# Chunked attention with a gated MLP on one core: scratch products ahead, row sums on TensorE, another order of loads

## The chip, the core and the metric

The kernel runs on one core of a Trainium2 chip (trn2). A core has TensorE (PE in the rows, with its weight loads as PEld), VectorE (DVE), ScalarE (ACT), GpSimd (POOL) and SyncE (SP), which here only starts transfers. Each engine works through its own queue in order and waits at the head of it. The metric is the device time of the one core in microseconds; lower is better.

## The reference

Attention first: each chunk of 32 queries sees 8 memory keys and the 56 keys from 16 before the chunk to 8 behind it, 64 in all.

```
scores = (q_c @ k_full.T) / sqrt(64)          # k_full: 8 memory keys, then 56 keys of the context
scores = scores - max(scores)
a      = exp(scores);  a = a / (sum(a) + 1e-9)
out_c  = a @ v_full
```

The heads are then put side by side (4 batches, 768 tokens, 512 columns), and a gated MLP follows:

```
h = relu(x @ w_in);  u, v = halves of h                     # 512 -> 1024
v = (v - mean(v)) / sqrt(var(v) + 1e-6)
g = u * (w_spatial @ v + b_spatial)                         # mixes the 768 tokens of a batch
out = g @ w_out                                             # 512 -> 512
```

Heads 8, head size 64. The MLP's weights arrive as 64-bit floats.

## The kernel before, in words

Attention runs in 24 units, six a batch: a unit is 4 chunks, so 128 queries, of all 8 heads. For unit i TensorE makes the scores (line L491, into the PSUM tile sx, of which there is one); DVE takes the row maximum (L558) and subtracts it into p (L562); ACT takes exp (L567); TensorE transposes p (L590, tile pt), ACT copies that to SBUF (L593, pT); TensorE multiplies with v (L491, "f<-vmain,pT", called P in the prediction, into a bank of tile f or into sx); DVE has meanwhile summed p and inverted the sum (L572, L573, L575) and scales the result into xs (L540 or L535); TensorE transposes it (L605, xt), ACT writes the high part of x (L610) and DVE the low part (L614). From unit 3 on (SPLIT) one burst makes the scores of unit i and the P of unit i-1 together.

The MLP's products carry each operand as a high and a low part (rounded to the type fp32r and the rest), so each product is three: the high parts of both (L642), the left one's low with the right one's high (L643), and the left one's high with the right one's low (L644); for v the left one is x, for u it is w_in. Such a triple is the unit of TensorE's work. For one token tile, v takes four triples of 512 columns ("f<-win_h,x", one for each 128 rows of w_in), u takes four triples of 384 columns for a block ("f<-x,win_h"), the token mixing takes six ("f<-wsp_h,vn") and the last product four ("f<-wout,big").

A block of 128 rows and 512 columns of w_in is converted from 64 bits by a chain over three engines: ACT takes the high word's value (L795) and the low word's (L800), DVE puts in exponent and sign (L804, L805), POOL adds (L810), ACT rounds to the high part win_h (L813), and DVE or POOL takes the low part win_l (L817). (c, 1) is the block of rows c for v, (c, 0) that for u. The raw blocks lie in tile big, with four buffers; a fifth load waits until the first buffer's add is done.

The operands of v come in two layers: 32 rows straight from memory, and 24 rows that are the next chunk's first rows, which for the first batch are copied on the chip by `shift_v` (L431, on ACT or POOL). P of a unit needs its copies.

`Plan` sets the order of everything. Each step is recorded with its engine (or a choice of engines with a cost for each), a cost, what it reads and writes, and a rank; the planner then lets time run, starts on each engine the step that can start first (the lowest rank among equals), and writes the instructions in that order. The order is fixed when the program is built; the hardware then waits by semaphores. The list FIRST gives the first loads in the order in which SP starts them, with conversion and load ranks for the w_in blocks. SP starts a load only when the loads ahead of it that are still under way would stay below AHEAD bytes.

The v of the MLP is normalized by POOL's power (L680), DVE's subtract and multiply (L684), ACT's rounding to the high part (L687) and DVE's low part (L691).

## Time and profile before

| | us |
|---|---|
| runs: median (lowest to highest, three) | 401.56 (400.12 to 403.46) |
| the profiled execution's own time | 403.73 |
| its span from first to last instruction | 402.0 |
| TensorE busy | 370.0 (92%) |
| DVE busy | 209.0 (52%) |
| ACT busy | 155.6 (39%) |
| POOL busy | 101.1 (25%) |

The busy shares are means over the whole span, and the span has two very different stretches. In the first 35 us data arrive, weights are converted and the first units pass through their chain, and TensorE has little to do; from about 92 us on TensorE works almost without a break. The table by stages in the prediction shows this. Of the profile's kinds of rows, those of the timeline give start, duration, engine, line and operation, and in brackets how long the engine stood idle before and what it waited for; those of groups give count, total busy time and the mean in ns.

### The profile page before, as it was taken

Reading aid. Unit: us, or ns where it says so; the run is one execution under the profiler, and the core shown is the slowest. Engines: PE = TensorE matmul, PEld = TensorE weight load, DVE = VectorE, ACT = ScalarE, POOL = GpSimd, SP = SyncE. Lnnn points to the kernel's source line nnn. Section 1 sums busy time; section 2 is a strip of 40 time slices with the busy share of each in tenths; the row PEclk is TensorE's granted clock in tenths of the full one; section 3 lists DMA queues with packets and bytes.
Section 4 is the critical chain, followed back from the end, with each engine's and each line's share of the span. In section 5 each row is a group of like instructions: output and inputs, shape, how many; then the busy total and the mean of one; then the engine's idle time right before and its main releaser. Section 6 shows DMA issues by size and latency. Waiting matters only on the chain.

```text
span 402.0 us, 11030 instructions
## 1 busy us (share of the span) xinstructions
PE 370.0 (92%) x4812; PEld 331.0 (82%) x4812; DVE 209.0 (52%) x401; ACT 155.6 (39%) x276; POOL 101.1 (25%) x114
## 2 busy tenths in 40 slices
PE   1458889889999999999999999999999999999996
PEld 0346777788989878889987988989989889899895
DVE  2799998897753525394661323475421324414040
ACT  6576765754342234344333222334211223321212
POOL 4786575332202101020121110110221201103031
PEclk9979999999999999999999999999999999999999
DMA  7889458861336450023736210000001020000202
GB/s 252 223 263 303 162 138 202 242 200 49 121 118 203 127 183 33 0 49 128 176 72 214 67 50 30 2 2 3 0 7 73 2 79 0 2 0 2 78 3 78
DMA packets 29505, 39.54 MB, mean 98 GB/s; under 512 B 5392, under 2 KB 23568, under 8 KB 29456
## 3 DMA queue, kind: packets, MB, share of 16 engines
q1 hardware_dynamic: 29152, 38.73, 32.1%
q8 instruction: 38, 0.62, 0.7%
q10 hardware_dynamic: 304, 0.10, 0.1%
q14 instruction: 11, 0.09, 0.1%
HBM read 32.52 MB, written 6.29 MB: 97 GB/s over the span
## 4 chain that ended last, share of the span: by engine, by line
PE 76%; DMA 13%; DVE 4%; ACT 3%; SPq 1%; issue 1%; POOL 1%; ACTq 0%; POOLq 0%
PE f L642 22%; PE f L644 22%; PE f L643 22%; PE sx L491 6%; DMA big<-in_moe_w_out_dram 3%; DMA big<-in_moe_w_in_dram 3%; DMA k<-in_k_dram 3%; PE xt L605 2%; PE pt L590 2%; DMA vmain<-in_mem_v_dram 1%; SPq L283 1%; DMA q<-in_q_dram 1%; DMA vmain<-in_v_dram 1%; DVE win_l L817 1%; POOL st L810 1%
## 5 line engine op out<-in xcount | busy, mean ns | idle before, releaser
L740 POOL TENSOR_TENSOR st<-st,u 128x384 f32<-128x384 f32 x32 | 33.7, 1056 | 141.9 <-DVE st L736 101.5
L642 PE MATMUL f<-wsp_h,vn 128*128 128x384 f32 x192 | 66.1, 344 | 0.0
L644 PE MATMUL f<-wsp_l,vn 128*128 128x384 f32 x192 | 64.5, 336 | 0.0
L643 PE MATMUL f<-wsp_h,vn 128*128 128x384 f32 x192 | 64.3, 335 | 0.0
L736 DVE TENSOR_TENSOR st<-f,bias 128x384 f32<-128x384 f32 x32 | 17.6, 553 | 54.5 <-PE f L644 54.4
L642 PE MATMUL f<-x,win_h 128*128 128x384 f32 x128 | 44.1, 345 | 0.5 <-issue 0.5
L643 PE MATMUL f<-x,win_l 128*128 128x384 f32 x128 | 43.0, 336 | 0.5 <-DVE win_l L817 0.5
L644 PE MATMUL f<-x,win_h 128*128 128x384 f32 x128 | 43.0, 336 | 0.0
L680 POOL TENSOR_TENSOR rstd<-ve,mhalf 128x1 f32<-128x1 f32 x24 | 15.5, 646 | 106.4 <-DVE ve L676 106.4
L743 ACT CAST big<-st 128x384 fp32r<-128x384 f32 x32 | 16.4, 512 | 64.5 <-POOL st L740 64.5
L642 PE MATMUL f<-win_h,x 128*128 128x512 f32 x96 | 39.6, 412 | 0.0
L644 PE MATMUL f<-win_l,x 128*128 128x512 f32 x96 | 37.9, 395 | 1.2 <-POOL k L261 1.2
L642 PE MATMUL f<-wout,big 128*128 128x512 f32 (+1 forms) x100 | 38.9, 389 | 0.0
L643 PE MATMUL f<-wout,big 128*128 128x512 f32 (+1 forms) x100 | 38.3, 383 | 0.0
L644 PE MATMUL f<-wout,big 128*128 128x512 f32 (+1 forms) x100 | 38.2, 382 | 0.0
L643 PE MATMUL f<-win_h,x 128*128 128x512 f32 x96 | 37.8, 394 | 0.0
L642 PEld LDWEIGHTS f<-wsp_h,vn 128*128 128x128 f32 x192 | 36.1, 188 | 1.3
L643 PEld LDWEIGHTS f<-wsp_h,vn 128*128 128x128 f32 x192 | 36.1, 188 | 0.7
L491 PEld LDWEIGHTS sx<-k,q 64*32 64x32 f32 x1536 | 17.6, 111 | 22.5 <-issue 12.5
L644 PEld LDWEIGHTS f<-wsp_l,vn 128*128 128x128 f32 x192 | 36.0, 188 | 0.0
L491 PE MATMUL sx<-k,q 64*32 64x64 f32 x1536 | 21.6, 235 | 15.5 <-POOL k L261 9.8
L672 DVE BATCH_NORM_STATS2 stats<-st 128x6 f32<-128x512 f32 x24 | 16.3, 681 | 27.8 <-ACT st L668 27.7
(75 smaller groups left out, 670.8 us busy)
## 6 DMA issues: line engine op xcount, KB each, us to landing
out_dram<-st SPq DMA_DIRECT2D x23, 256.0 KB
k<-in_k_dram SPq DMA_DIRECT2D x7, 800.0 KB
q<-in_q_dram SPq DMA_DIRECT2D x7, 768.0 KB
vmain<-in_v_dram SPq DMA_DIRECT2D x38, 128.0 KB
big<-in_moe_w_in_dram SPq DMA_DIRECT2D x8, 512.0 KB
vmain<-in_v_dram SPq DMA_DIRECT2D x35, 96.0 KB
big<-in_moe_w_spatial_dram SPq DMA_DIRECT2D x6, 384.0 KB
big<-in_moe_w_out_dram SPq DMA_DIRECT2D x4, 512.0 KB
```

What stands on the lines that cost most here:

```text
L283: me["ins"] = e.dma_start(out=dst() if callable(dst) else dst, in_=src_).ins
L491: nc.tensor.matmul(o, w_, m, start=True, stop=True, skip_group_check=True)
L590: nc.tensor.transpose(a[:, t], p[:, t], ident)
L605: nc.tensor.transpose(a[:, t], xs[:, t], ident)
L642: nc.tensor.matmul(o, lh, rh, start=(j == 0), stop=False)
L643: nc.tensor.matmul(o, ll, rh, start=False, stop=False)
L644: nc.tensor.matmul(o, lh, rl, start=False, stop=(j == len(pairs) - 1))
L672: nc.vector.bn_stats(stats, t_["st", s])
L680: nc.gpsimd.tensor_tensor(a, t_["ve", i], mhalf, op=ALU.pow)
L736: nc.vector.tensor_tensor(alloc("st", s_, [P, HT], F32), t_["f", n], bias[:, tok], op=ALU.add)
L740: nc.gpsimd.tensor_tensor(a, a, t_["u", i], op=ALU.mult)
L743: nc.scalar.copy(t_["g", i][:, 0, 0:HT], t_["st", s_])
```

## The change

The new program differs in these points.

- The low parts of w_in and w_out (L817) are now always POOL's (WLOW has only POOL); before, DVE or POOL took them.
- The sums of p of units 0, 1 and 2 are made by TensorE: four products of the transposed p with a matrix `halves` of two columns put the sums of the two heads of a pair beside the unit's P in the same PSUM bank. DVE adds the small constant and inverts (`recip`); its reduction (L572) is left out for these three units.
- The first batch's six normalizations of v are done by ACT (an activation with scale and bias) in place of DVE; DVE makes the bias (`shifts`), one column.
- 28 scratch products of 512 columns (`heat`), whose result nobody reads, stand in TensorE's queue among the first units: 7 ahead of unit 0's scores, 4 behind them, 10 behind unit 1's scores, 7 behind unit 1's transpose.
- SPLIT is 3, so that the scores of unit 3 and P of unit 2 are two steps.
- The first loads come in another order, v in pieces of 3, 1 and 2 units (before 2, 1, 2 and 1), AHEAD is 2,000,000; two of the blocks of w_in are converted only behind the step p of unit 0 and of unit 4 (gate). The copies of keys may go to ACT in the first batch.
- The planner's costs differ, it models a slow and a fast clock of TensorE (`Clock`), and so all orders move.
- Functions with the conditions PSUB and XLOW (both 0) make no instructions. The transposes of xs are written as products with the transpose flag; they are the same four instructions.

TensorE's queue at the start of the program, before. In the names pt is the transposed p, sx the scores, xt the transposed xs; "f<-vmain,pT" is P.

```order
L491 MATMUL sx<-k,q 32x64 x64
L590 MATMUL pt<-ident,p 128x128 x4
L491 MATMUL sx<-k,q 32x64 x32
L590 MATMUL pt<-ident,p 128x128 x4
L491 MATMUL f<-vmain,pT 32x64 x64
L605 MATMUL xt<-ident,xs 128x128 x4
L590 MATMUL pt<-ident,p 128x128 x4
L642 MATMUL f<-win_h,x 128x512
```

The same place now, from the first scratch product to P of unit 1; "xt<-minus" is a scratch product and "f<-halves,pT" the sums of p.

```order
L306 MATMUL xt<-minus 128x512 x7
L546 MATMUL sx<-k,q 32x64 x32
L306 MATMUL xt<-minus 128x512 x4
L682 MATMUL pt<-ident,p 128x128 x4
L546 MATMUL sx<-k,q 32x64 x32
L306 MATMUL xt<-minus 128x512 x10
L546 MATMUL sx<-k,q 32x64 x32
L546 MATMUL f<-halves,pT 128x2 x4
L546 MATMUL f<-vmain,pT 32x64 x32
L682 MATMUL pt<-ident,p 128x128 x4
L306 MATMUL xt<-minus 128x512 x7
L546 MATMUL f<-halves,pT 128x2 x4
```

Before, the scores of units 0 and 1 stood together ahead of unit 0's transpose; now unit 1's scores stand behind it, and the scratch products lie between.

POOL's queue from its first add to the low part of the last of v's four blocks, before. st_233 is block (0,1), st_243 (3,1), st_319 (2,1), st_257 (1,1).

```order
L810 TENSOR_TENSOR st_233<-st_233,big_148 128x512
L431 COPY vmain_113<-vmain_113 24x4x256 x2
L810 TENSOR_TENSOR st_243<-st_243,big_184 128x512
L431 COPY vmain_113<-vmain_113 24x4x256 x2
L810 TENSOR_TENSOR st_319<-st_319,big_236 128x512
L810 TENSOR_TENSOR st_257<-st_257,big_192 128x512
L360 MEMSET k1_143 128x4x16
L484 COPY k_429<-memT_112 128x16x8
L261 COPY k1_143<-k1_143 128x16x24
L817 TENSOR_TENSOR win_l_108<-st_257,win_h_107 128x512
```

The same place now, without its first three rows (the adds of st_219 and st_227 and one copy of 24x4x192). st_227 is block (0,1), st_219 (1,1), st_279 (3,1), st_276 (2,0), st_459 (2,1).

```order
L486 COPY vmain_113<-vmain_113 24x4x256
L935 TENSOR_TENSOR win_l_108<-st_227,win_h_107 128x512
L486 COPY vmain_113<-vmain_113 24x4x192
L415 MEMSET k1_158 128x4x16
L928 TENSOR_TENSOR st_279<-st_279,big_214 128x512
L935 TENSOR_TENSOR win_l_108<-st_219,win_h_107 128x512
L935 TENSOR_TENSOR win_l_108<-st_279,win_h_107 128x512
L928 TENSOR_TENSOR st_276<-st_276,big_208 128x512
L928 TENSOR_TENSOR st_459<-st_459,big_294 128x512
L539 COPY k_569<-memT_112 128x16x8
L935 TENSOR_TENSOR win_l_108<-st_276,win_h_107 128x512
L935 TENSOR_TENSOR win_l_108<-st_459,win_h_107 128x512
```

Of the low parts of v's blocks POOL had one and now has all four, and a fifth, of u's block (2,0), stands ahead of the last of them.

The diff, cut to its core:

```diff
-AHEAD = 1800000
-SPLIT = 2
-FIRST = [("qk", 0, (0, 0), 1), ("qk", 0, (1, 2), 2), ("mem", 0, "ACT", True), ("w", 0, 1, -6.0, 2.0),
...
+AHEAD = 2000000
+SPLIT = 3
+FIRST = [("qk", 0, (0, 0), 1), ("mem", 0, "ACT", True), ("qk", 0, (1, 2), 2), ("w", 1, 1, 40.0, 3.0),
+         ("w", 0, 1, -39.0, 2.0), ("w", 2, 0, 50.0, 27.0), ("w", 3, 1, 49.0, 5.0, 0), ("v", 0, 3, False),
...
+HOT = (7, 4, 3, 7, 7, 0, 0)
+PSUMS = 3
+VACT = 6
-KEYS = {"POOL": 0.43}
-WLOW = {"DVE": 0.62, "POOL": 1.26}
+KEYS = {"ACT": 0.42, "POOL": 0.43}
+WLOW = {"POOL": 1.35}
...
+    for r in range(2):
+        nc.vector.memset(halves[:, r:r + 1], 0.0)
+        nc.vector.memset(halves[r * D:(r + 1) * D, r:r + 1], 1.0)
     nc.scalar.activation(warm, mhalf, AF.Exp)
+    nc.scalar.activation(minus, ident, AF.Copy, scale=-1.0)
...
+    def heat(n, r=()):
+        def go():
+            if ("xt", "warm") not in t_:
+                alloc("xt", "warm", [P, 512], F32, psum=True)
+            for _ in range(n):
+                nc.tensor.matmul(t_["xt", "warm"], minus, minus.unsqueeze(1).broadcast_to([P, T, P]), start=True, stop=True, skip_group_check=True)
+        if n:
+            op("PE", 0.233 * n, go, r=r, w=[("xt", "warm")], rank=99.0, tail=0.25, count=2 * n)
...
+                    if part == "p" and i - 1 < PSUMS:
+                        for t in range(T):
+                            mm(t_["sum", i - 1][:, 2 * t:2 * t + 2], pT[:, t], halves)
...
+    def recip(i, rank, banks):
+        def go():
+            d = small.tile([P, T * 2], F32, tag="den", name="den")
+            nc.vector.tensor_tensor(d, t_["sum", i], tiny, op=ALU.add)
+            rec = t_["rec", i] = small.tile([P, T, 2], F32, tag="rec", name="rec")
+            nc.vector.reciprocal(rec.rearrange("p t r -> p (t r)"), d)
...
+        def shifts():
+            a = t_["shift", i] = small.tile([P, 1], F32, tag="shift", name="shift")
+            nc.vector.scalar_tensor_tensor(a, t_["mvar", i][:, 0:1], -1.0, t_["rstd", i], op0=ALU.mult, op1=ALU.mult)
+
+        def norm_act():
+            a = t_["st", s]
+            nc.scalar.activation(a, a, AF.Identity, bias=t_["shift", i], scale=t_["rstd", i])
...
-    def w_in_part(c, part, rank, load_rank):
+    def w_in_part(c, part, rank, load_rank, gate=None):
...
+        for convert in held.get(i, ()):
+            convert()
```

More of the change, by code (lines that the diff above doesn't have):

```diff
@@ L34, with __init__, roll, of @@
 VLATE = 0
-VNORM = {"DVE": 0.5}
-VLOW = {"DVE": 0.61}
-KEYS = {"POOL": 0.43}
-WLOW = {"DVE": 0.62, "POOL": 1.26}
-SHIFT = {"POOL": 1.0, "ACT": 1.0}
-SPREAD = {"ACT": 2.6, "POOL": 3.0}
+PSUB = 0
+XLOW = 0
+PSUMS = 3
+VACT = 6
+VNORM = {"DVE": 0.6}
+VLOW = {"DVE": 0.85}
+KEYS = {"ACT": 0.42, "POOL": 0.43}
+WLOW = {"POOL": 1.35}
+SHIFT = {"POOL": 1.08, "ACT": 0.95}
+SPREAD = {"ACT": 2.6, "POOL": 3.0}
+class Clock:
+    def __init__(self, phase):
+        self.end, self.k, self.busy = phase, 2.0, 0.0
+    def roll(self, t):
+        while t >= self.end:
+            if self.k == 2.0 and self.busy >= 2.5:
+                self.k = 1.0
+            elif self.k == 1.0 and self.busy < 1.4:
+                self.k = 2.0
+            self.busy, self.end = 0.0, self.end + SHORT
+    def of(self, t):
+        self.roll(t)
+        return self.k
+    def work(self, a, b, heat):
+        self.roll(a)
+        while b > self.end:
+            self.busy += heat * (self.end - a)
+            a = self.end
+            self.roll(a)
+        self.busy += heat * (b - a)
 class Plan:
@@ L88, in order @@
         end, ready = self.end, self.start = {}, {}
-        free = {e: 0.0 for e in ENGINES}
+        free = {e: 0.75 if e in ("SP", "ACT") else 0.0 for e in ENGINES}
+        clock = Clock(CLOCK0)
         pipe, lanes, begun, fetched = 0.0, [], 0, {}
@@ L136, in order @@
                 begun, us = begun + count, at - t
+                clock.work(t, at, heat)
             self.on[n] = e
@@ L563, in sub, with less, exp_less @@
                                     t_["mx", i].unsqueeze(3).broadcast_to([P, 2, T, WIN]), op=ALU.subtract)
+        def less():
+            for r in range(2):
+                nc.tensor.matmul(t_["scores", i][:, r], minus.bitcast(F32),
+                                 t_["mx", i][:, r].unsqueeze(2).broadcast_to([P, T, WIN]), start=False, stop=True,
+                                 skip_group_check=True)
+        def exp_less():
+            p = alloc("p", i, [P, T, 2, WIN], F32)
+            nc.scalar.activation(p.rearrange("p t r w -> p r t w"), t_["scores", i], AF.Exp, scale=scale)
         def exp():
@@ L579, in softmax @@
            w=[sx, ("mx", i)], rank=rank)
-        op("DVE", dve(512), sub, r=[sx, ("mx", i)], w=[("p", i)], rank=rank)
-        op("ACT", act(512), exp, w=[("p", i)], rank=rank)
-        op("DVE", dve(512) + 0.36, den, r=[("p", i)], w=[("rec", i)], rank=rank + 0.6)
+        if i < PSUB:
+            op("PE", 0.95, less, r=[("mx", i)], w=[sx], rank=rank, tail=0.25, count=8)
+            op("ACT", act(512) + 0.03, exp_less, r=[sx], w=[("p", i)], rank=rank)
+        else:
+            op("DVE", dve(512), sub, r=[sx, ("mx", i)], w=[("p", i)], rank=rank)
+            op("ACT", act(512), exp, w=[("p", i)], rank=rank)
+        if i >= PSUMS:
+            op("DVE", dve(512) + 0.38, den, r=[("p", i)], w=[("rec", i)], rank=rank + 0.6)
     def flip(i, rank):
@@ L617, in flip, with rest, low_copy @@
             op("ACT", act(512), high, r=[("xt", j)], w=[("x", n, tt, "h")], rank=rank + 0.5)
-            op("DVE", dve(512), low, r=[("xt", j), ("x", n, tt, "h")], w=[("x", n, tt, "l")], rank=rank + 0.5)
+            def rest():
+                a = t_["xt", j].rearrange("p t q -> p (t q)")
+                nc.tensor.matmul(a, minus, t_["x", n][:, 0, :, o:o + UT], start=False, stop=True, skip_group_check=True)
+            def low_copy():
+                nc.scalar.copy(t_["x", n][:, 1, :, o:o + UT], t_["xt", j])
+            if j < XLOW:
+                op("PE", 0.3, rest, r=[("x", n, tt, "h")], w=[("xt", j)], rank=rank + 0.5, tail=0.25, count=2)
+                op("ACT", act(512), low_copy, r=[("xt", j)], w=[("x", n, tt, "l")], rank=rank + 0.5)
+            else:
+                op("DVE", dve(512), low, r=[("xt", j), ("x", n, tt, "h")], w=[("x", n, tt, "l")], rank=rank + 0.5)
     def attend(i, rank):
@@ L694, in ffn_v @@
         rank += VLATE if b == 0 else 0
-        op("DVE", 0.85, stat, r=[k_], w=[("ve", i)], rank=rank)
+        op("DVE", 1.0, stat, r=[k_], w=[("ve", i)], rank=rank)
         op("POOL", 0.6, power, r=[("ve", i)], w=[("rstd", i)], rank=rank)
-        op(VNORM if b == 0 else {"DVE": 0.5}, 0, norm, r=[("rstd", i)], w=[k_], rank=rank)
+        if i < VACT:
+            op("DVE", 0.15, shifts, r=[("rstd", i)], w=[("shift", i)], rank=rank)
+            op("ACT", act(512) + 0.2, norm_act, r=[("shift", i)], w=[k_], rank=rank)
+        else:
+            op(VNORM if b == 0 else {"DVE": 0.5}, 0, norm, r=[("rstd", i)], w=[k_], rank=rank)
         op("ACT", act(512), high, r=[k_], w=[("vn", i, "h")], rank=rank)
```

74 lines of the change are left out of this document (51 added, 23 removed), and 7 rows, old and new, of the table FIRST.

## The prediction

> **What bounds the kernel now.** I read first the table of busy time by stages over the span of 402.0 us (columns: stretch, length, busy time of PE, PEld, DVE, ACT, POOL, clock, DMA share, GB/s).
>
> ```profile
> 0.00:29.00 29.00, 9.88 (x337) 7.59 (x337) 18.73 (x31) 18.36 (x24) 19.89 (x25) 0.93 0.83 244
> 29.00:35.00 6.00, 4.79 (x140) 3.73 (x139) 5.84 (x13) 4.30 (x7) 4.54 (x6) 0.78 1.00 291
> 35.00:92.00 57.00, 51.20 (x872) 43.77 (x872) 52.33 (x93) 37.59 (x69) 29.74 (x27) 1.00 0.68 195
> 92.00:402.00 310.00, 304.10 (x3467) 275.96 (x3467) 132.06 (x267) 95.33 (x177) 46.90 (x58) 1.00 0.21 63
> ```
>
> From 92 us on TensorE is busy for 304.1 of 310 us: it is the bound there, and only its own work or its 5.9 us of idle time could shorten that stretch. The change does neither. Up to 29 us TensorE works for 9.9 us. From 35 to 92 us DVE is the fullest engine (52.3 of 57), and TensorE has 5.8 us of idle time. So the time is the moment at which TensorE's dense work starts, plus its waits up to 92 us, plus a stretch that stays. I read that moment in TensorE's timeline (start, duration, operation, idle time ahead in brackets):
>
> ```profile
> 28.16 1.11 PE L590 MATMUL pt<-ident,p 128*128 128x128 f32 x4 [1.61 <-ACT p L567]
> ...
> 29.50 0.63 PE L643 MATMUL f<-win_h,x 128*128 128x512 f32 x1
> 29.93 0.63 PE L644 MATMUL f<-win_l,x 128*128 128x512 f32 x1
> ...
> 34.93 0.40 PE L644 MATMUL f<-win_l,x 128*128 128x512 f32 x1 [1.21 <-POOL k L261]
> ...
> 35.86 0.39 PE L642 MATMUL f<-win_h,x 128*128 128x512 f32 x1
> ...
> 36.55 0.40 PE L642 MATMUL f<-win_h,x 128*128 128x512 f32 x1
> ...
> 38.38 0.60 PE L590 MATMUL pt<-ident,p 128*128 128x128 f32 x4
> ...
> 40.29 0.86 PE L491 MATMUL sx<-k,q 64*32 64x64 f32 x64
> ...
> 41.72 0.50 PE L642 MATMUL f<-win_h,x 128*128 128x512 f32 x1
> ```
>
> The last stall of the head ends at 34.93, in the third product of v's second triple. From there a triple takes 36.55 - 35.86 = 0.69 us, and a burst of scores and P 41.72 - 40.29 = 1.43. The clock is read from durations: four transposes take 1.11 us at 28.16 and 0.60 at 38.38, and products follow each other at 0.43 us (29.50, 29.93) and later at 0.23. TensorE is at about half pace until some 32 us.
>
> The waits behind the head are in the view of waits, TensorE's alone from 34.5 to 92 us (total, times, longest):
>
> ```profile
> PE xt L605 <- DVE xs L535: 2.0, 3, 1.1
> PE pt L590 <- ACT p L567: 1.5, 1, 1.5
> PE sx L491 <- issue: 1.4, 1, 1.4
> ...
> PE f L643 <- DVE win_l L817: 0.5, 1, 0.5
> ```
>
> **The change, part by part.**
>
> *Start of the dense work.* The prices of the conversion chain and of what shares its queues are in the groups by line up to 92 us (count, busy total, mean in ns, idle time):
>
> ```profile
> L810 POOL TENSOR_TENSOR st<-st,big 128x512 uint32<-128x512 uint32 x12 | 16.9, 1414 | 19.1 <-ACT x L610 7.0 <-ACT pT L593 3.5 <-ACT big L800 2.2
> L431 POOL COPY vmain<-vmain 24x1024 f32<-24x1024 f32 x4 | 5.2, 1306 | 0.9 <-DMA vmain<-in_v_dram 0.8
> L680 POOL TENSOR_TENSOR rstd<-ve,mhalf 128x1 f32<-128x1 f32 x6 | 3.8, 633 | 6.5 <-DVE ve L676 6.4
> ...
> L261 POOL COPY k<-k 128x384 f32<-128x384 f32 x6 | 3.1, 519 | 2.9 <-DMA k<-in_k_dram 2.9
> L431 POOL COPY v<-v 24x768 f32<-24x768 f32 x2 | 1.6, 820 | 0.1
> ...
> L817 POOL TENSOR_TENSOR win_l<-st,win_h 128x512 fp32r<-128x512 f32 x1 | 1.3, 1278 | 0.0
> ```
>
> In the new order PE's third triple needs the low part of block (2,1), and that is POOL's last of a long row. POOL's first add waits for ACT's low word, behind unit 0's pT copy; before, the corresponding step stands here, and v's first rows arrive just behind it:
>
> ```profile
> 15.23 0.67 ACT L800 ACTIVATE big<-big 128x512 uint32<-128x512 uint32 x1
> 16.88 2.87 POOL L431 COPY vmain<-vmain 24x1024 f32<-24x1024 f32 x2 [0.76 <-DMA vmain<-in_v_dram]
> 10.00:20.00 10.00, 4.15 (x136) 3.33 (x136) 7.68 (x11) 5.86 (x10) 7.90 (x7) 1.00 0.82 222
> ```
>
> I take 15.23 + 0.67 = 15.9 for the new start too. From there to the low part of (2,1) POOL has five adds (5 x 1.414 = 7.07), five low parts (5 x 1.278 = 6.39), copies of v (1.306 + 2 x 0.82 = 2.95) and two small steps (no price here, taken as 0.5): 16.9 us. The copies come after two adds, at 18.7. But v is now loaded behind four blocks of w_in (before three), and as three units in place of two: 0.52 + 0.26 MB more ahead of it, at 222 GB/s some 3.5 us, less where transfers overlap; I take 3.2. It arrives at about 20.0, and POOL waits 1.3 us. End: 15.9 + 16.9 + 1.3 = 34.1. By then PE has done one triple (0.69) and one group of four transposes (0.45, since its 0.60 above overlaps with what follows) more than before at 34.93. Advance: 34.93 - 34.1 + 1.14 = **2.0 us**. Other ends: no wait for v, 3.3; rows of POOL at their longest, a loss (below).
>
> The chain of the first units is not what ends last any more, so their gains are hidden. ACT used to keep unit 0's exp behind two loads:
>
> ```profile
> 11.58 0.68 ACT L795 ACTIVATE st<-big 128x512 f32<-128x512 f32 x1 [2.51 <-DMA big<-in_moe_w_in_dram]
> 12.70 0.64 ACT L567 ACTIVATE p<-p 128x512 f32<-128x512 f32 x1
> 20.30 1.18 PE L491 MATMUL f<-vmain,pT 64*32 64x64 f32 x64
> ```
>
> Now it stands ahead of them. But P of unit 0 needs v, at 20.0 and a copy later, so it does not start before the 20.3 us or so that it had; unit 1's exp stands on ACT behind those copies. The 28 scratch products cost 28 x 0.43 = 12.0 us at half pace, 28 x 0.23 = 6.4 at full pace. TensorE is idle for 29 - 9.9 = 19 us of that stretch, which covers them. Without that cover they are in front of the scores in the queue: seven (3.0 us) fit before the keys of unit 0 are there, and I put 0 to 0.4 us on that step, off the path. The twelve sum products of two columns hide in the same idle time; they take three of DVE's reductions away (below 0.7 us each), also ahead of the bound. SPLIT, AHEAD and the copies of keys on ACT (0.52 us each off POOL) act on the same first chain and count nothing more.
>
> *A second passage through POOL.* From 34.1 to the low part of (0,0) POOL has two adds, two copies of v, one of 768, power, keys, the low part and a small step: 2.83 + 2.61 + 0.82 + 0.63 + 0.52 + 1.28 + 0.15 = 8.8, so 42.9. PE reaches u's first triple after nine triples, three groups of transposes and a burst: 34.1 + 6.2 + 1.35 + 1.43 = 43.1. It is covered, by 0.2 us, and if it were not, each 0.1 us of POOL costs as much. The last block (3,0) comes behind another low part, power, an add and a piece of w_spatial, some 6 to 7 us on; PE then has a burst and twelve triples of u (0.69 x 384 / 512 = 0.52 each), 7.7 us, so this is covered as well.
>
> *Waits from 35 to 92 us.* What DVE loses:
>
> ```profile
> L817 DVE TENSOR_TENSOR win_l<-st,win_h 128x512 fp32r<-128x512 f32 x7 | 6.3, 898 | 0.0
> L817 DVE TENSOR_TENSOR wout<-st,wout 128x512 fp32r<-128x512 f32 x4 | 3.8, 964 | 1.0 <-ACT wout L813 0.8
> L684 DVE TENSOR_SCALAR st<-st,mvar,rstd 128x512 f32<-128x512 f32 x6 | 3.8, 627 | 0.1
> 79.93 0.69 DVE L817 TENSOR_TENSOR wout<-st,wout 128x512 fp32r<-128x512 f32 x1 [0.84 <-ACT wout L813]
> 80.54 0.68 DVE L562 TENSOR_TENSOR p<-sx,mx 128x512 f32<-128x512 f32 x1
> ```
>
> Four of the seven win_l lie behind 34.9 us (4 x 0.90), and all of wout (3.8) and the normalizations (3.8): 11.2 us, less the six shifts of one column (no row; 0.2 each, and at most a pass of 0.7), so some 10 off 52.3. The three waits for xs (2.0) and the one for win_l (0.5) are DVE's, and the 1.5 us for exp begins with a DVE that stood at wout (79.93) with the subtraction behind it (80.54); wout is now POOL's. I let these 4.0 us go. The 1.4 us of "issue" stays, since no engine releases it. ACT takes six normalizations (no such row; ACT's passes over 512 columns above take 0.64 and 0.68; with two operands of one column a little more is possible, and nothing less than half; I take 0.65, 3.9 us), from 37.6 to 41.5 of 57. Its queue can then make exp wait; I book one new wait of the mean size of those for xs, **0.7 us**. Net 3.3.
>
> *Behind 92 us:* same products, 0.
>
> *Sum.* 2.0 + 4.0 - 0.7 = 5.3 us: a span of 396.7, an own time of 403.73 - 5.3 = 398.4, and against the median 401.56 - 5.3 = **396.3 us**. (The profiled execution lay 2.2 us over the median; runs ranged from 400.12 to 403.46.)
>
> A row that speaks against giving POOL more to do, the same DVE step beside an idle and beside a working POOL:
>
> ```profile
> 83.37 0.37 DVE L804 TENSOR_SCALAR st<-st 128x512 uint32<-128x512 uint32 x1
> 85.00 1.28 DVE L804 TENSOR_SCALAR st<-st 128x512 uint32<-128x512 uint32 x1
> 84.60 1.31 POOL L810 TENSOR_TENSOR st<-st,big 128x512 uint32<-128x512 uint32 x1 [7.04 <-ACT x L610]
> ```
>
> The second ran until 86.28, 0.37 us behind the end of POOL's add (85.91): it stood still until POOL was done. The Trainium skill, "SBUF — State Buffer", section "Who interferes with whom", calls the port pair of the two engines an exclusive lock under which the second to issue fully blocks; the trace agrees, 0.91 + 0.37 = 1.28. So every low part that moves to POOL can also hold up DVE, and DVE can hold up POOL. That is the slow rival.
>
> **The rivals.**
>
> 1. *POOL becomes the bound (slower).* For: two passages with 1.3 us and 0.2 us of play, and adds that take up to 1.74 where DVE stands in their way:
>
> ```profile
> L810 POOL TENSOR_TENSOR st<-st,big x6: 1281/1304/1739, 14.8 to 39.2; 128x512 uint32<-128x512 uint32 x6
> ```
>
> At 1.74 - 1.30 = 0.44 more for each of the ten adds and low parts, (2,1) comes 4.4 us later, the passage to (0,0) loses another 4 x 0.44 - 0.2 = 1.6, and DVE's relief is eaten: 6.0 - 2.0 = 4.0 us slower, 405.6, and with (3,0) late too 406. Against: the median add is 1.30. It decides from a mean of about 1.6 us a step.
>
> 2. *The waits stay.* SP starts batch 1's memory rows, and v behind them, only when its earlier loads have found buffers:
>
> ```profile
> 55.52 4.02 SPq L283 DMA_DIRECT2D vmain<-in_mem_v_dram  x8
> ```
>
> The buffers come from POOL's work on w_spatial, which is not earlier. A TensorE that is ahead then waits for these. Only the head's advance is left: 399.6.
>
> 3. *Everything fits.* POOL doesn't wait for v (3.3) and all 5.8 us of idle time go: 9.1, so 392.5. Against: the "issue" wait.
>
> 4. *The scratch products don't hold the clock.* Between them TensorE is still idle for some 3 us at a time. If the dense work starts at half pace for as long as before (28.16 to about 32, some 4 us), that costs 2 us: 398.3. The Trainium skill, "TensorE: Matmul & The Clock Gate", "Part 1: The HAM clock gate", has a free-running window of about 3.4 us, full rate after a busy one, half after an idle one. By it the gaps matter; that the clock rose after some 4 us of work here agrees.
>
> **Numbers.** Chances: forecast 0.50 (394 to 398.5), rival 1 0.10, rival 2 0.22, rival 3 0.12, rival 4 0.06. A measurement of this kernel tells about 1% (4.0 us) from no change. Faster, below 397.5: 0.42 of the forecast, rival 3, a little of rival 4: 0.56. Slower, above 405.6: most of rival 1, 0.08. Between: 0.36. The range goes from rival 3 less 0.5 to rival 2 plus 1.4 for the spread of its runs: 392.0 to 401.0, leaving out rival 1 and the tails.
>
> **What would show it.** The low part of block (2,1) on POOL ends near 34 us and the third triple's last product follows at once; a win_l or add of over 1.6 us would speak for rival 1. TensorE's idle time from 35 to 92 us falls from 5.8 to near 2.5 us, with no wait on xs or win_l left; 5 us or more, ending on v's transfers, is rival 2. Transposes at 20 to 30 us take 0.6 us, not 1.11. Behind 92 us idle time stays near 5.9. A long wait of ACT for a transfer at the head of its queue, which the sum doesn't have, would make it wrong.

## The result, and the profile after

The changed kernel takes 399.52 us (median of 20 runs, 396.52 to 403.48); the kernel before, run beside it, takes 403.0 (20 runs, 399.73 to 406.89). The ratio is 0.9935, 95% interval 0.9911 to 0.9959: 0.65% faster, or 2.6 us. (A ratio leaves out runs of more than 1.5% above their kernel's fastest, so it need not be the quotient of the medians.) In two more comparisons below it is 0.9896 (0.9861 to 0.9931) and 0.9901 (0.9868 to 0.9935). The forecast was 396.3 us and a gain of 5.3; by the medians the gain is 3.5, inside the 1% to which the prediction gave a chance of 0.36, and by the ratio it is about half of the forecast. Of the miss in the time, 1.4 us is the median of before, which more runs put at 403.0 in place of 401.56.

The profiled execution's own time is 398.16, its span 396.1, so 5.9 less than the span before. The stages (columns as in the prediction's table):

```profile
0.00:29.00 29.00, 22.23 (x380) 17.28 (x380) 13.92 (x29) 20.89 (x29) 19.41 (x24) 0.82 0.88 269
29.00:35.00 6.00, 3.99 (x140) 3.41 (x139) 3.95 (x10) 3.35 (x7) 4.51 (x5) 0.84 0.93 254
35.00:92.00 57.00, 56.67 (x906) 50.84 (x906) 47.39 (x92) 45.17 (x77) 38.18 (x33) 0.99 0.63 186
92.00:397.00 305.00, 300.91 (x3443) 272.76 (x3441) 130.42 (x265) 95.65 (x177) 48.16 (x59) 1.00 0.22 64
```

From 35 to 92 us TensorE's idle time fell from 5.8 to 0.33 us. Behind 92 us it fell from 5.9 to 396.1 - 92 - 300.91 = 3.2, of which 3.1 lie behind the last product. The view of waits has one TensorE wait left from 35 to 92 us and none behind:

```profile
PE sx L546 <- issue: 0.3, 1, 0.3
```

TensorE's timeline where the dense work starts:

```profile
30.83 0.42 PE L546 MATMUL f<-vmain,pT 64*32 64x64 f32 x23
33.26 0.93 PE L546 MATMUL f<-vmain,pT 64*32 64x64 f32 x41 [2.01 <-issue]
34.12 0.79 PE L748 MATMUL f<-win_h,x 128*128 128x512 f32 x1
34.71 0.63 PE L749 MATMUL f<-win_h,x 128*128 128x512 f32 x1
35.13 0.63 PE L750 MATMUL f<-win_l,x 128*128 128x512 f32 x1
...
38.03 0.40 PE L750 MATMUL f<-win_l,x 128*128 128x512 f32 x1
```

In the middle of P of unit 2 TensorE stood still for 2.0 us, waiting for nothing that the profile shows. Its next products followed each other at 0.42 us, half pace, and the third triple's last product began at 38.03. POOL's row ended where the prediction had it: the low parts of (2,0) and (2,1), two in the second line below, were done at 31.64 + 2.49 = 34.13 (34.1 forecast). That is in part luck, since its first add began at 14.32 (15.9 forecast), v's rows were there at 19.00 (20.0 forecast), and the rest of the row was that much longer.

```profile
19.00 2.43 POOL L486 COPY vmain<-vmain 24x768 f32<-24x768 f32 x2 [1.95 <-DMA vmain<-in_v_dram]
...
31.64 2.49 POOL L935 TENSOR_TENSOR win_l<-st,win_h 128x512 fp32r<-128x512 f32 x2
```

So the head came out 2.0 us worse than no change (the same amount of work would have stood at 34.93 + 1.14 = 36.07), and the waits behind it 8.2 us better (5.8 - 0.33, and 5.9 - 3.2). 8.2 - 2.0 = 6.2 is the 5.9 of the two spans within 0.3.

### The profile page after: what moved, and what is told of

It reads as the page before. It is cut to its first block, busy times and chain, and to the rows that moved or that the text cites. A ratio compares the mean times of both kernels' runs of the same rounds, so it can differ in the third digit from the quotient of the medians.

```text
span 396.1 us, 11126 instructions
## 1 busy us (share of the span) xinstructions
PE 383.8 (97%) x4864; PEld 344.3 (87%) x4864; DVE 195.7 (49%) x392; ACT 165.1 (42%) x289; POOL 110.3 (28%) x119
## 4 chain that ended last, share of the span: by engine, by line
PE 91%; DMA 7%; issue 1%; POOL 1%; SPq 0%; ACT 0%; POOLq 0%
PE f L748 26%; PE f L749 25%; PE f L750 25%; PE sx L546 8%; DMA vmain<-in_v_dram 3%; PE xt L699 3%; PE pt L682 3%; DMA big<-in_moe_w_in_dram 1%; PE f L546 1%; DMA k<-in_k_dram 1%; DMA vmain<-in_mem_v_dram 1%; PE xt L306 1%; POOL vmain L486 1%; SPq L338 0%; ACT st L890 0%
## 5 line engine op out<-in xcount | busy, mean ns | idle before, releaser
L786 POOL TENSOR_TENSOR rstd<-ve,mhalf 128x1 f32<-128x1 f32 x24 | 16.6, 691 | 102.2 <-DVE ve L782 102.2
L865 DVE TENSOR_TENSOR big<-st,big 128x384 fp32r<-128x384 f32 x32 | 20.6, 645 | 21.9 <-ACT big L861 21.6
L890 ACT COPY st<-f 128x512 f32<-128x512 f32 (+1 forms) x25 | 14.2, 571 | 31.3 <-PE f L750 30.9
```

The source lines that it names most:

```text
L786: nc.gpsimd.tensor_tensor(a, t_["ve", i], mhalf, op=ALU.pow)
L865: nc.vector.tensor_tensor(a[:, 1, 0:HT], t_["st", s_], a[:, 0, 0:HT].bitcast(F32), op=ALU.subtract)
L890: nc.scalar.copy(alloc("st", s_, [P, N], F32), t_["f", n])
```

## The experiments

Ratios are to the kernel before, run beside each; each is given with its 95% interval.

### What holds TensorE at the start of the dense work

The theory, A: that wait is for TensorE's own program, which arrives piece by piece, and its cost grows because TensorE's clock is at half pace in the window behind it. The rivals: B, the profiled execution was an odd one and POOL's row ends the head; C, the scratch products are the gain of the change; D, the larger AHEAD is.

*The changed kernel once more.*

> The changed kernel once more, as the neighbour for the three below and for a second profile. All theories: 0.990 to 0.996 of the kernel before. Theory A (the head's gain is lost to TensorE's own instruction stream: at its 475th product, the 23rd of P of unit 2, it has no further instructions and stands still for some 2 us, and the clock gate then gives half pace for one window): a wait of 1.5 to 2.5 us ended by 'issue' at the 475th product, and the triples behind it at 0.43 us a product if a window of the gate falls into it. Rival B (the profiled execution was an odd one, and POOL ends the head as the prediction had it): no such wait, and the third triple ends with block (2,1)'s low part near 34 us.

397.48 us, 0.9896 (0.9861 to 0.9931). The wait is there again, 1.4 us, at the same place, when TensorE has begun 475 products of its program (the expectations call this the 475th product), and the third triple's last product begins at 37.69, 3.6 us behind the end of POOL's row (34.14). B falls.

*The scratch products left out, order kept.*

```diff
-            for _ in range(n):
-                nc.tensor.matmul(t_["xt", "warm"], minus, ...)
+            pass
```

> All 28 scratch products left out, everything else and every order kept. Theory A: the wait stays at the 475th product, which is now 28 products later in the work (the 51st of P of unit 2), so the stall is where it was in time to within 1 us, the clock is half behind it either way, and the time is that of the changed kernel within 1 us (0.25%). Rival C (the scratch products are what gains): the first units run at half pace, dense work starts 2 to 4 us later, and the time is 2 to 4 us above the changed kernel, about that of the kernel before.

399.36 us, 0.9931 (0.9900 to 0.9962). From TensorE's timeline, P of unit 2 and the end of the third triple:

```profile
32.79 0.46 PE L546 MATMUL f<-vmain,pT 64*32 64x64 f32 x17
34.11 0.34 PE L546 MATMUL f<-vmain,pT 64*32 64x64 f32 x13 [0.86 <-issue]
...
37.20 0.40 PE L750 MATMUL f<-win_l,x 128*128 128x512 f32 x1
```

13 of P's 64 products are left behind the wait, 41 in the changed kernel: it moved 28 products on within P, and so stays behind the 475th product of the program. TensorE was at half pace until 31.8 us and at full pace from then on, and the triples ended 0.5 us sooner than in the execution above. By the ratios the scratch products are worth 0.35% (1.9 us by the medians), with intervals that overlap. That is more than A expected (1 us at most) and at the lower edge of C's 2 to 4 us. Most of the gain stands without them: C, as the whole of the gain, falls; that they are worth something is neither shown nor excluded.

*The scratch products with 8 columns instead of 512.*

```diff
-nc.tensor.matmul(t_["xt", "warm"], minus, minus.unsqueeze(1).broadcast_to([P, T, P]), ...)
+nc.tensor.matmul(t_["xt", "warm"][:, 0:8], minus, minus[:, 0:8], ...)
```

> The 28 scratch products stay but write 8 columns in place of 512: the same number of instructions, hardly any activity. Theory A: the wait stays at the 475th product, 23rd of P of unit 2, as in the changed kernel; half pace up to some 33 us at least; time within 1 us of the changed kernel. Rival C: 2 to 4 us above it, as without scratch products. If this one and the one without scratch products differ by more than 1 us, the place of the instruction wait matters more than the clock.

398.53 us, 0.9922 (0.9891 to 0.9954). TensorE's timeline:

```profile
33.30 1.24 PE L546 MATMUL f<-vmain,pT 64*32 64x64 f32 x64
34.47 0.79 PE L748 MATMUL f<-win_h,x 128*128 128x512 f32 x1
35.06 0.63 PE L749 MATMUL f<-win_h,x 128*128 128x512 f32 x1
```

At half pace P of unit 2 starts so late that the program is there, and there is no wait, where A expected one; the first triple starts at 34.47 all the same (34.12 in the changed kernel's profile). The time is 1.05 us above the unchanged kernel's by the medians, at the edge of what A allowed.

*AHEAD as before.*

```diff
-AHEAD = 2000000
+AHEAD = 1800000
```

> AHEAD back at 1,800,000 bytes, the rest of the change kept (a few orders on ACT and POOL move with it, TensorE's not). Theory A with the addition that the instruction load waits behind the data loads that are under way: the wait at the 475th product shrinks from 2.0 to 1.8 us or less, and the time falls by 0 to 1 us. Rival D (loads further ahead are a gain of the change): v and the blocks of w_in land later, the time rises by 0.5 to 2 us.

397.44 us, 0.9897 (0.9854 to 0.9940): D falls. The wait was 1.9 us here, in the slowest of the six executions, and not shorter as expected, so that the data loads under way hold the program's load back is not shown.

### Undoing one part, with the order planned anew

The second question is where the 8.2 us behind the head come from. Theory R is the prediction's: DVE was relieved. Its rival O: the order that the planner wrote, with the list of loads that belongs to it.

*The normalization back on DVE* (`VACT = 6` becomes `VACT = 0`).

> The changed kernel with the six normalizations of the first batch back on DVE (a subtract and multiply of 512 columns, 0.63 us each, in place of a shift of one column); planned anew, all else as changed. TensorE's idle time from 35 to 92 us was 5.8 us before the change and 0.33 after. Theory R (the gain between 35 and 92 us is DVE's relief: with 47.4 of 57 us it no longer ends TensorE's waits): DVE gets 6 x (0.63 - 0.2) = 2.6 us back, ACT loses some 4; half a microsecond to 1.5 us of idle time returns on steps of DVE, the ratio to before rises by 0.1 to 0.4% against the unchanged kernel (0.990 to 0.994). Theory O (the gain comes from the order of the loads and steps, whoever does the work): idle time stays under 0.6 us and the ratio is that of the unchanged kernel, 0.990 to 0.9935, with less than 0.1% of difference to be had. TensorE's wait for nothing the profile shows stays at its 475th product, since the same instructions stand ahead.

399.9 us, 0.9938 (0.9902 to 0.9973); idle time from 35 to 92 us 1.4 us. The wait behind the 475th product was 0.5 us here, and no half-pace window followed it. Some 0.4% slower than the unchanged kernel by the ratios, with intervals that overlap: as R has it, at the edge of what can be told.

*The low parts to be had by DVE or POOL again.*

```diff
-WLOW = {"POOL": 1.35}
+WLOW = {"DVE": 0.62, "POOL": 1.26}
```

> The changed kernel with the low parts of w_in and w_out to be had by DVE or POOL again, at the costs of before; planned anew. Theory R: up to 10 us of work go back to DVE's queue, idle time of TensorE from 35 to 92 us rises from 0.33 to 2 to 4 us, ended by xs, exp or win_l, and the time by 0.4 to 1.0% against the unchanged kernel (ratio to before 0.995 to 1.000). Theory O: idle time under 1 us, ratio 0.989 to 0.994. In both the head ends at the same moment, since TensorE's 475th product stands where it stood, though the low part of (2,1) is no longer the last of a row on POOL.

411.64 us, 1.0230 (1.0177 to 1.0282), far more than either theory gave. Its stage from 35 to 92 us:

```profile
35.00:92.00 57.00, 50.26 (x860) 42.35 (x859) 47.80 (x92) 41.85 (x73) 33.02 (x30) 0.99 0.66 193
```

6.7 us of idle time, with a DVE that is no fuller than in the changed kernel (47.80 against 47.39), so R can't explain it. One row of the view of waits, for 92 us on, shows the largest, which neither theory has, keys on ACT:

```profile
PE sx L546 <- ACT k L316: 4.9, 2, 3.3
```

*The sums of p by DVE* (`PSUMS = 3` becomes `PSUMS = 0`).

> The changed kernel without the twelve products that sum p of units 0 to 2; DVE's three reductions are back; planned anew. TensorE's product number 475 now stands 12 products further on, inside P of unit 2 (its 36th of 64 in place of the 24th). If the wait there is TensorE's program being loaded, it moves to that place, 12 products on, and the first triples end within 0.5 us of where they were (37.7 to 38.0 for the last of the third). If it were a wait for v's copies, it would stay at the 24th. DVE gets 3 x 0.6 us more in the head, which nobody waits for: idle time from 35 to 92 us within 0.8 us of the changed kernel, ratio to before 0.989 to 0.994 by both theories; above 0.995 the sums are worth something.

404.46 us, 1.0050 (1.0011 to 1.0089). TensorE's timeline at the wait and behind it:

```profile
33.09 0.35 PE L546 MATMUL f<-vmain,pT 64*32 64x64 f32 x17 [2.76 <-issue]
...
36.84 1.11 PE L682 MATMUL pt<-ident,p 128*128 128x128 f32 x4 [0.81 <-ACT p L654]
```

17 products of P's 64 are left behind the wait, so it moved on by 24 and not by twelve: the twelve sums run as 24 products (4,864 in the changed kernel, 4,840 here). With that it stands behind the 475th again. Two half-pace windows follow, from 34.65 to 41.48 us. How much of the 0.5% is these and how much is the sums, this run doesn't tell.

*The list of first loads and AHEAD of before.*

> The changed kernel with the list of first loads and the limit of bytes under way of before (no block held back behind a step p); sums, normalization, low parts on POOL and scratch products stay; planned anew. Theory O: the gain goes, idle time of TensorE from 35 to 92 us is 3 to 6 us again, ended by steps that wait for loads or for POOL, ratio to before 0.997 to 1.003. Theory R: idle time stays under 1.5 us and the ratio is 0.990 to 0.995. The 475th product stands in the same place of P of unit 2 and waits for its instructions again, unless v's copies, which come ahead of the blocks, make P of unit 2 late themselves.

409.6 us, 1.0190 (1.0143 to 1.0238). Idle time from 35 to 92 us is 5.2 us, with 45.85 us of work on DVE, less than in the changed kernel. TensorE's waits there:

```profile
PE pt L682 <- ACT p L654: 3.0, 1, 3.0
PE xt L699 <- DVE xs L604: 1.4, 1, 1.4
PE xt L699 <- DVE x L709: 0.8, 2, 0.5
```

All of DVE's relief is in this kernel, and the gain is gone, as O has it. But the ratio lies above O's range too (0.997 to 1.003), so the order written anew may have cost something by itself (see below).

### Undoing or doing one part with the order kept

*The twelve low parts issued to DVE, every other queue row for row the same.*

```diff
-            (nc.vector if e == "DVE" else nc.gpsimd).tensor_tensor(l_, ...)
+            nc.vector.tensor_tensor(l_, ...)
```

> The changed kernel with its order kept on every engine, but the twelve low parts of w_in and w_out issued to DVE at the places in time where POOL has them (0.9 us each on DVE, 10.8 us in all, some 8 of them from 35 to 92 us); POOL's queue loses them, TensorE's and ACT's are the same row for row. Theory R (the gain from 35 to 92 us is DVE's relief): DVE goes from 47.4 to some 55 of 57 us there, TensorE's idle time from 0.33 to 3 to 6 us, ended by xs, p, x or win_l, ratio to before 0.997 to 1.005. Theory O (it is the order, not the engine): idle time under 1.2 us, ratio 0.989 to 0.994, better if POOL's shorter row lets the triples of the head start earlier (they don't, if TensorE's program sets that: the wait at the 475th product stays).

400.01 us, 0.9934 (0.9906 to 0.9962). From 35 to 92 us:

```profile
35.00:92.00 57.00, 54.43 (x892) 47.72 (x891) 49.96 (x95) 42.91 (x75) 30.61 (x26) 1.00 0.61 184
```

2.6 us of idle time (2.0 of it for xs), between the two expectations; the ratio lies in O's range (0.989 to 0.994), at its upper edge. In this execution there was hardly a wait for the program (0.24 us), the third triple's last product began at 35.74, 2.0 to 3.2 us ahead of the unchanged kernel, and the span still was 397.1: the waits for xs and the rest took all of it back.

*The low parts on POOL in the kernel before, its order kept*: one part of the change alone (the same line, `nc.gpsimd` in place of the choice).

> The kernel before with its order kept on every engine, but the eleven low parts that DVE had issued to POOL at the same places: this part of the change alone. Theory R: DVE's 52.3 of 57 us fall to some 47, the waits for xs (2.0 us) and win_l (0.5) go, TensorE's idle time from 35 to 92 us is 2 to 4 us in place of 5.8, ratio to before 0.991 to 0.996, unless low parts of 1.3 us on POOL come late for the triples. Theory O: POOL's queue, whose order was not made for them, puts new waits in their place: idle time of 5 us or more, ratio 0.998 to 1.010.

405.1 us, 1.0069 (1.0037 to 1.0101): slower. The waits for xs didn't go, and POOL's came on top:

```profile
PE pt L590 <- ACT p L567: 3.1, 1, 3.1
PE xt L605 <- DVE xs L535: 2.1, 2, 1.2
PE f L644 <- POOL st L810: 1.3, 1, 1.3
PE f L643 <- POOL win_l L817: 1.2, 2, 0.9
```

DVE had 47.97 us of work from 35 to 92 us in place of 52.33 and its waits stayed: relief without an order made for it is worth less than nothing.

*Both parts of DVE's relief undone, order kept*: the low parts as above, and the normalization as DVE's subtract and multiply at the places of ACT's.

> The changed kernel with its order kept, and with both things that DVE was relieved of issued to DVE again: the twelve low parts of w_in and w_out (0.9 us each) and the six normalizations (0.63 us each; the shifts of one column stay). TensorE's rows are the same. Theory R (DVE's relief is the gain from 35 to 92 us): DVE is as full there as before the change, 52 to 56 of 57 us, TensorE's idle time is back at 4 to 6 us, ratio to before 0.998 to 1.006. Theory O (the order that the planner wrote is the gain, and the engine matters little as long as its queue is not full): idle time 1.5 to 3.5 us, ratio 0.992 to 0.997.

405.8 us, 1.0056 (1.0019 to 1.0092). TensorE's rows are those of the changed kernel, and the gain is gone. The stage from 35 to 92 us:

```profile
35.00:92.00 57.00, 52.12 (x868) 45.15 (x867) 51.28 (x96) 37.50 (x67) 29.13 (x25) 0.97 0.64 191
```

And TensorE's waits in it:

```profile
PE xt L699 <- DVE xs L604: 4.1, 3, 2.1
PE pt L682 <- ACT p L654: 0.5, 1, 0.5
PE sx L546 <- issue: 0.3, 1, 0.3
```

The idle time is 4.9 us, and a half-pace window (56.5 to 59.9 us) stands right behind the wait of 2.1. The 601st product begins 3.6 us ahead of the unchanged kernel's in the same comparison (39.37 against 42.98) and the span ends 2.8 behind (400.4 against 397.6): 6.4 us lost to DVE behind the head. R is right here, given this order: both parts on DVE cost some 1.5% by the ratios (1.0056 against 0.9901). One part alone costs 0.3 to 0.4% (0.9934 for the low parts; 0.9938 for the normalization, in a kernel that was planned anew), with intervals that overlap the unchanged kernel's. The profiled execution took 402.23 us, 3.6 below the median, so its waits don't account for the whole 1.5%.

*Nothing undone, one number of the planner changed that no instruction carries.* First the time it counts for a load to land (2.0 becomes 1.95):

> The changed kernel with one number of the planner changed that no instruction carries: the time it counts for a load to land is 1.95 us in place of 2.0. The same work on nearly the same engines and the same order of loads, but TensorE's and ACT's queues are written in another order from the first units on. Theory O (the result hangs on the order as such, and the list of loads fits one order): time moves by more than the measurement's 0.35%, ratio to before 0.994 to 1.020, with 2 us or more of idle time from 35 to 92 us. Rival (orders written from nearly the same costs are worth the same, and the losses of the runs that were planned anew come from what they changed): ratio 0.988 to 0.994, idle time under 1.5 us.

0.9973 (0.9923 to 1.0024). Its twelve runs lie from 397.56 to 406.52 us with a median of 404.54, and the interval reaches into both expectations: this run decides nothing. (Its profiled execution, at 405.02 us, has 4.6 us of idle time in that stretch, 4.2 of it one wait of the "issue" kind.) Then ACT's cost for a column (0.00095 becomes 0.00094):

> The changed kernel with another number of the planner changed that no instruction carries: ACT's cost for a column is 0.00094 in place of 0.00095 us. The same work, another order on every engine, and some of the later loads in another order. Theory O: ratio to before 0.994 to 1.020, idle time of TensorE from 35 to 92 us 2 us or more. Rival: 0.988 to 0.994, idle time under 1.5 us.

412.72 us, 1.0231 (1.0187 to 1.0276). The same products, and in the stage from 35 to 92 us DVE has only 42.5 us of work:

```profile
35.00:92.00 57.00, 51.18 (x853) 43.81 (x851) 42.48 (x86) 41.16 (x72) 34.21 (x30) 0.91 0.64 186
```

TensorE's waits in it, for xs, exp and its program:

```profile
PE xt L699 <- DVE xs L604: 2.0, 1, 2.0
PE pt L682 <- ACT p L654: 2.0, 1, 2.0
PE sx L546 <- issue: 1.0, 1, 1.0
```

The idle time is 5.8 us, and four half-pace windows (31.24 to 38.06 and 61.96 to 68.78 us) lie in the stage or over its start. Another order alone, of the steps and of some later loads, costs 3.3% against the changed kernel (1.0231 to 0.9901), three times the gain of the change. So the loss of a kernel that was planned anew (vact0, wlow, psums0, oldfirst) says little about the part that was undone in it.

*The changed kernel beside these.*

> The changed kernel once more, beside the other three on the same chip: ratio to before 0.989 to 0.995 by all theories. The wait at TensorE's 475th product is 0.2 to 2 us, and what it takes (with the half-pace window behind it, if there is one) is found again at the end of the span to within 0.3 us, if nothing behind the head has time to spare.

398.79 us, 0.9901 (0.9868 to 0.9935). Its wait behind the 475th product was 2.2 us with two half-pace windows from 31.68 on. Three executions of the changed kernel show what such a head costs: the 601st product begins at 41.75, 42.09 and 42.98 us, and the spans are 395.5, 396.1 and 397.6. A head that is 0.34 and 1.23 us late is 0.6 and 2.1 late at the end: nothing behind it makes it good. The first agrees with the expectation (within 0.3 us); the second lost 0.9 us more, to waits further on.

### Two more on the head

*Ten scratch products moved to where TensorE waits.* Order and count kept: none ahead of unit 0's scores or behind its transpose, ten behind P of unit 1.

> The changed kernel with its order kept, but of the 28 scratch products the first seven and the three behind unit 0's transpose are left out, and ten stand behind P of unit 1 instead, just ahead of the place where TensorE waits for its program. As many products stand ahead of the 475th as now. Theory A (that product waits for its instructions whatever stands ahead, and the idle window of the clock that the wait makes costs as much again): the ten products (2.3 us at full pace) run while the instructions are on their way, the wait shrinks from 1.4 to 2.0 us to under 1 us, no half-pace window follows it, and the third triple's last product ends at 36.0 to 37.0 us in place of 37.7 to 38.0; ratio 0.985 to 0.991. Rival: the ten products delay the loading as well, or what follows waits for POOL's low parts at 34.1: the third triple ends at 37.5 or later, ratio 0.989 to 0.995.

398.62 us, 0.9915 (0.9885 to 0.9946). The head did what A said, no wait and no half pace:

```profile
33.00 0.94 PE L550 MATMUL f<-vmain,pT 64*32 64x64 f32 x64
33.87 0.50 PE L755 MATMUL f<-win_h,x 128*128 128x512 f32 x1
...
36.70 0.39 PE L757 MATMUL f<-win_l,x 128*128 128x512 f32 x1
...
37.74 0.50 PE L756 MATMUL f<-win_h,x 128*128 128x512 f32 x1 [0.41 <-DVE x L716]
```

The third triple's last product is 1.0 to 2.2 us ahead of the unchanged kernel's, and none of it reaches the end (span 396.9): the next wait is DVE's x at once, and 0.8 us more are a wait of the "issue" kind behind the 982nd product. The ratio lies just above A's range (0.985 to 0.991), in its rival's. A head that is a microsecond or two faster meets the next queue.

*The kernel before, a second profiled execution.*

> The kernel before, unchanged, with a second profiled execution, to see what of its first is its own. If the waits belong to the program: idle time of TensorE from 35 to 92 us 5 to 6.5 us, behind 92 us 5 to 6.5, span 400 to 402.5, and the wait at the 473rd product again, of 0.5 to 2 us, with the half-pace time of the clock ending within 3.4 us of 31.6. If the first execution was an odd one, these differ by more than 1.5 us.

Span 399.4, against 402.0 in the first. From 35 to 92 us:

```profile
PE sx L491 <- issue: 2.0, 3, 1.2
PE xt L605 <- DVE xs L535: 1.7, 2, 1.1
PE f L644 <- POOL v L431: 1.4, 1, 1.4
PE f L643 <- DVE win_l L817: 0.5, 1, 0.5
PE pt L590 <- ACT p L567: 0.4, 1, 0.4
```

In the head it is up to 1.1 us ahead of the first, until both wait behind the 473rd product and go on at 34.86 and 34.93; at the 1,201st they still agree to 0.1 us. The wait for exp is 0.4 in place of 1.5, and idle time behind 92 us is 4.5 in place of 5.9. So 2.6 of the 5.9 us between the first pair of spans belonged to one execution of before; 399.4 - 396.1 = 3.3 is close to the 3.5 of the medians.

## Why the prediction was wrong, and where it was right

**Start of the dense work (+2.0): this step failed.** The sum of POOL's row was right to 0.1 us, but nothing waited for it. The failing sentence is "PE's third triple needs the low part of block (2,1), and that is POOL's last of a long row", taken as what ends the head. Two kernels that have this row on POOL, and a wait of 0.5 us at most, began the third triple's last product at 36.62 and 36.70 (vact0, hotlate), 1.3 and 0.6 us behind the end of POOL's row (35.31 and 36.08); the three executions of the changed kernel, with 1.4 to 2.2 us of waiting and half pace behind it, at 37.69, 38.03 and 38.91. Against 36.07 the step was -2.0 us in the profile, -1.6 and -2.8 in the other two. The sign was in the profile of before: the row at 34.93 names a copy of keys as releaser, which that product doesn't read, and the same wait in the second execution names a copy of v.

Even those two lie 0.6 us behind 36.07. What ends the head there is the path that the prediction had set aside: "The chain of the first units is not what ends last any more, so their gains are hidden." In the changed kernel's profile the chain of work that ended last, followed back from the dense work, is TensorE's own row from P of unit 0 on, which starts when POOL's copy of v is done:

```profile
20.39 1.04 POOL vmain L486
21.44 0.04 issue
21.48 1.16 PE f L546 x59
22.65 1.04 PE pt L682 x4
23.69 2.83 PE xt L306 x7
26.52 1.57 PE f L546 x61
...
29.91 1.35 PE f L546 x31
31.25 2.01 issue
```

TensorE works without a break from 21.48 to 31.25 us, up to 26.2 us at half pace, and then stands still for 2.0 us. So the step lacked two things: TensorE's own row of the first units, and the wait in it.

What it waits for stands in the records of transfers. The page has one queue of instruction loads, in before and after alike:

```profile
q8 instruction: 38, 0.62, 0.7%
```

That is 38 loads of 16,384 bytes, 0.62 MB, for the 4,864 products of the changed kernel: on average one load for 128 products. The loads that end ahead of the waits (from the trace's records; us):

```
run                 load starts  ends    products begun   next one begins   behind the load's end
before              32.08        33.23   472 (+1 at once) 34.93             1.70
before, second      32.39        33.46   473              34.86             1.40
low parts on POOL   32.67        33.73   473              35.22             1.49
after               30.65        31.81   475              33.26             1.45
again               29.99        31.21   475              32.80             1.59
again2              30.66        31.68   475              33.08             1.40
sums by DVE         30.71        31.68   475              33.09             1.41
before, "issue"     73.74        75.27   1232             76.63             1.36
before, 2nd         74.04        74.98   1232             76.35             1.37
normal. on DVE      30.45        31.62   447 (+28 first) 33.16             1.54
no scratch          31.30        32.62   444 (+31 first) 34.11             1.49
```

Where TensorE has used up what is there, it goes on 1.36 to 1.70 us behind the end of the load. In the last two lines it was still 28 and 31 products away when the load ended; it made these first, and then it too waited behind the 475th, until 1.5 us behind the load's end. Of the 18 profiled executions 15 have a wait at this place (behind the 473rd to 475th product), of 0.24 to 2.8 us; in the other three (short, hotlate, alldve) TensorE came there 1.56 us or more behind the load's end and did not wait. The wait behind the 982nd product, in four executions, lies 507 products further on, five short of four times 128, and ends 1.35 to 1.49 us behind a load. That the load is the cause is inferred from this regularity and from the wait's move by 28 and by 24 products in the experiments; no run changed the loading itself.

**Cost of the scratch products (0 to 0.4).** Too small, and not off the path: the seven behind unit 1's transpose (2.83 us) stand in the rows above. ACT had the transposed p of unit 1 ready at 25.57, and TensorE came to the products that read it at 26.36, up to 0.8 us later. This does not show in the dense work, since the wait for the program follows: without the scratch products it is 0.86 us in place of 2.0. Their worth is not shown to be more than nothing. "Transposes at 20 to 30 us take 0.6 us": unit 1's took 1.11, unit 2's 0.60; the clock came and went (next section).

**Waits from 35 to 92 us (3.3).** 5.5 in the first pair, 4.6 - 0.33 = 4.3 with before's second execution. The waits for xs, win_l and exp went, as said; the "issue" wait, which the prediction kept because no engine releases it, went too, since in the new order TensorE doesn't outrun its program at that place; and the new wait of 0.7 never came. The mechanism, DVE's relief, holds in the new order (alldve: 1.0056), but its larger part, the low parts, doesn't hold by itself (lowpool: 1.0069, slower). The step left out that the gain needs an order made for it. In that stretch DVE fell by 4.9 us where some 10 were forecast (52.33 to 47.39); over the whole span it fell by 13.3, from 209.0, as the page's line of busy times shows:

```profile
PE 383.8 (97%) x4864; PEld 344.3 (87%) x4864; DVE 195.7 (49%) x392; ACT 165.1 (42%) x289; POOL 110.3 (28%) x119
```

**Behind 92 us (0).** 2.7 us in the first pair, 4.5 - 3.2 = 1.3 with the second execution: waits for keys, and waits of the "issue" kind, that before has there and after hasn't.

**The rivals.** POOL is not the bound: its adds take 1.399 us on average and its low parts 1.287 and 1.454, below the 1.6 from which the rival decides. TensorE waits for no load of v (rival 2). Rival 4's 2 us for a lost clock came true in part, from a cause it didn't know: the half-pace window behind the wait.

**The sum.** 2.0 + 3.3 + 0 was forecast; the better pair of spans (before's second execution) gives -2.0 + 4.3 + 1.3 = 3.6, the medians 3.5. The step that was wrong by 4 us was offset, by some 2.3 us, by two that were too small: that the total came within 1.7 us of the forecast is luck.

## What to carry to other kernels

Where many small products of TensorE stand together, count them: a wait that the profile calls "issue", or puts down to a step the product doesn't read, is worth checking against the instruction loads, and it moves with the number of products and not with the data. Where a planner writes the order, undo a part with the order kept before judging it, since here an order written anew from nearly the same costs lost up to 3.3%. And take a second execution of the kernel before when the forecast rests on single waits: 2.6 us of them were one execution's own.

## What the runs showed of the hardware

TensorE's program came in 16,384-byte loads during the execution, and in the head, with the data loads under way, TensorE had to wait 0.24 to 2.8 us behind its 473rd to 475th product in 15 of 18 executions. That it waited for a load is inferred, as said above.

The clock changed only at the edges of windows of 3.413 us, whose phase differs between executions of the same kernel (from the trace's clock records; us):

```
after         full 9.14-12.55, half -15.97, full -19.38, half -26.21, full -33.03, half -36.45, full to the end
again2        full 7.79-11.20, half -14.61, full -21.44, half -24.85, full -31.68, half -38.51, full -396.90
noscratch     half to 31.77, full -397.00
hotlate       full 8.67-12.08, half -15.49, full -18.91, half -25.73, full -397.79
```

In the changed order and its variants half pace came during or behind waits in the head of 0.8 to 2.8 us (after, again, again2, ahead18, psums0, wlow), and not behind those of 0.24, 0.49 and 0.86 us (lowdve, vact0, noscratch). So a window in which TensorE is idle for part of the time can be enough (1.4 us in again), where the prediction speaks of an idle one. By an estimate from the window's length, each half-pace window that lies over dense work costs up to 3.41 / 2 = 1.7 us, so a stall of 2 us can cost nearly four. The Trainium skill, "TensorE: Matmul & The Clock Gate", "Part 1: The HAM clock gate", calls the window free-running and the ramp's cost below 1% of a span; the phases above agree with the first, and the 0.35% for the scratch products is in keeping with the second.
